# Unit 1's keys ahead of the last two weight conversions, and TensorE in source order from unit 1 on, in a fused complex-decay attention and gated feed-forward kernel

## The chip, the cores and the metric

The kernel runs on one core of one Trainium2 chip. The metric is the device time of one execution in microseconds; the time before is 690.07 us, the median of three runs (689.92 to 690.43). The engines are named as the profile names them: PE is TensorE (PEld its weight loads), DVE is VectorE, ACT is ScalarE, POOL is GpSimd, SP is SyncE, which here only issues DMAs.

## The reference, cut to what matters

```
batch, n_heads, seq, head_dim = (4, 8, 768, 48)
n_tokens, d_model, d_ff = (3072, 384, 1536)
...
mag = np.sqrt(a_re * a_re + a_im * a_im)
scale = np.minimum(mag, 0.999) / (mag + 1e-06)
a_re_n, a_im_n = (a_re * scale, a_im * scale)
for t in range(S):
    new_re = ar * S_re - ai * S_im
    new_im = ar * S_im + ai * S_re
    kv = np.einsum('bhd,bhe->bhde', k[:, :, t], v[:, :, t])
    S_re, S_im = (new_re + kv, new_im)
    y[:, :, t] = np.einsum('bhd,bhde->bhe', q[:, :, t], S_re)
...
a = x @ w_a
b = x @ w_b
return (a * b @ w_out).astype(np.float32)
```

A linear attention whose state is multiplied by a complex decay at each token; its output, 384 wide per token, goes through a gated feed-forward layer of 1536 hidden columns. Everything is fp32.

## The kernel before

**Units.** The 3072 tokens are cut into 12 units of 256 (two batches by a chunk of 128 tokens). Units 0 to 5 are the six chunks of the first pair of batches, 6 to 11 those of the second; a unit carries on the state of the one before it in its six.

**prep(u)**, on DVE with help from ACT, turns the decays of unit u into products over the chunk: about 45 small and large DVE operations in one chain (L205 to L348). In it, scale(u + 1) (L172) prepares the next unit's decays. At its end the queries are multiplied by the products P (times_p, L314) and the keys by a reciprocal (L337), then the second half of times_p follows (for units under LED the query half comes ahead of the reciprocal). stack(u) (L353) then copies queries and keys from the tile qk to the tile stk, ten DMAs on SP's queue a time; for the units under EARLY the query half is stacked in a round of its own, ahead of the keys. load_qk (L350) fetches the next unit's queries and keys into qk after that.

**attn(u)** is PE work: scores (L396), masked by DVE into a tile am (L399); transposes of the keys (L407), copied by ACT into kt (L411); outputs (L436), split by ACT and DVE into two parts xh (L440) and xl (L445); state (L452), added by DVE (L459). A unit in the middle of its six has 2 x 2 scores, 2 x 2 transposes, 2 x 2 outputs and 2 states. They are traced in bundles: the list `order` in attn has a None where one ends. The PSUM tiles of scores, transposes and states take turns on three banks ("m"); am and kt have two buffers each.

**The feed-forward part.** In "window" w, the loop over w at L683, unit w's hidden columns are worked in 12 blocks, k = 0 to 11, two at a time: 36 matmuls of the first layer per pair (L498), the product a*b split into hh and hl by ACT and DVE (L502 to L505, `gated`), and 12 matmuls of the second layer (L534), which lag by one pair. The bundles of attn(w + 1) are traced in the same loop, each after one of the k that SLOTS lists for this w. prep(w + 2) is traced in slices of 2400 ns a k; in window 0 all of prep(2) is traced at k = 11.

**The weights** come as 64-bit numbers and are converted in 12 blocks of three parts, 36 in all: three DVE operations (L142, L144, L146) build a fp32 value in a tile of the name o_sb (three buffers), ACT writes its high part (L150), PE two matmuls with the identity (L152, L153) give the remainder in PSUM, and ACT writes that (L154). Blocks 0 to 5 are traced ahead of unit 0's attention (CONV_FIRST), blocks 6 to 11 in window 0, one a k: at each k the conversion comes first, then a slice of prep(1), and at k = P1_AT = 4 the rest of prep(1), stack(1), eight matmuls of the identity with qk that nothing reads (WARM, L702), load_qk(2).

**What sets the order.** A scheduler reorders each engine's instructions when the kernel is built: what is traced earlier has priority, `high_priority` lifts some of it (the gated operations by 4000, masks and copies of attention by 2000), and a schedule by estimated durations fixes the order. On the chip each engine then runs its own list strictly in that order. Within `tc.manual_schedule(engines={pe.engine})` (L691), PE's list is the order of the source; before, this holds from window w = 4 on (`w + 1 == LED`, LED = 5).

## Time and profile before

| what | value |
|---|---|
| median of three runs | 690.07 us |
| the profiled execution | 688.8 us |
| its span, first to last instruction | 687.1 us |
| granted TensorE clock over the span | 0.974 |
| PE busy | 643.3 us |
| DVE busy | 542.3 us |
| ACT busy | 288.8 us |

A line of a view gives start or group, busy time, count, and in brackets the idle time of that engine just before with what ended it. PE and DVE both run close to without a break from 60 us on; which of them the other waits for differs from stage to stage, so the rows below go by stage.

### The profile page before, as it was taken

The numbers are of one execution on the slowest core, as the hardware profiler recorded it, in microseconds if no ns is written. First come the engines' busy times: TensorE is split into PE (matmuls) and PEld (weight loads), VectorE is DVE, ScalarE is ACT, GpSimd is POOL, SyncE is SP. The second block draws the span as 40 slices with busy tenths as digits, with TensorE's granted clock in tenths as the row PEclk, the third lists the DMA queues.
The fourth block names the chain that finished last, engine by engine and source line by source line (L and its number), as shares of the span: only waits on it lengthen the run. The fifth ranks groups of instructions, "written<-read, shape, count | busy, mean of one in ns | idle before, by whom it ended". The sixth has DMA issues, their size and how long they took to land.

```text
span 687.1 us, 14031 instructions
## 1 busy us (share of the span) xinstructions
PE 643.3 (94%) x5854; PEld 605.4 (88%) x5854; DVE 542.3 (79%) x1069; ACT 288.8 (42%) x472; POOL 5.6 (1%) x11
## 2 busy tenths in 40 slices
PE   3647999999999999999999899999999999999996
PEld 1214889898999999999999899999999899999996
DVE  6999999999989999999998989989989644223221
ACT  7357754634545255352454635346141422221211
POOL 3000000000000000000000000000000000000000
PEclk9577999999999999999999999999999999999999
DMA  8973201512314234061430701520600500400000
GB/s 310 403 297 97 103 1 29 158 55 83 118 37 142 62 100 124 18 183 42 116 123 1 210 30 47 134 75 32 164 29 6 156 32 6 119 24 2 24 1 28
DMA packets 32086, 63.91 MB, mean 93 GB/s; under 512 B 3985, under 2 KB 10641, under 8 KB 32017
## 3 DMA queue, kind: packets, MB, share of 16 engines
q1 hardware_dynamic: 28560, 58.23, 27.3%
q10 hardware_dynamic: 3456, 4.72, 1.9%
q8 instruction: 48, 0.79, 0.5%
q14 instruction: 22, 0.17, 0.1%
HBM read 39.32 MB, written 4.72 MB: 64 GB/s over the span
## 4 chain that ended last, share of the span: by engine, by line
PE 48%; DVE 34%; DMA 7%; ACT 5%; issue 4%; SPq 1%; DVEq 0%; ACTq 0%
PE ab L498 26%; PE o L534 12%; DMA w<-in_dram 5%; PE pm L396 4%; DVE a_t L295 4%; PE xp L436 3%; DVE qk L315 3%; DVE h_t L503 2%; PE pm L452 2%; DVE hl L505 2%; DVE pr L232 2%; DVE z L300 2%; DMA stk<-qk 2%; DVE pr L262 2%; DVE am L399 2%
## 5 line engine op out<-in xcount | busy, mean ns | idle before, releaser
L498 PE MATMUL ab<-xh,w 128*128 128x256 f32 x1728 | 322.5, 281 | 0.1
L498 PEld LDWEIGHTS ab<-xh,w 128*128 128x128 f32 x1728 | 269.8, 188 | 2.1 <-issue 0.6
L498 PE MATMUL ab<-xl,w 128*128 128x256 f32 x864 | 242.1, 280 | 0.2
L498 PEld LDWEIGHTS ab<-xl,w 128*128 128x128 f32 x864 | 162.3, 188 | 1.4 <-DVE xl L445 1.1
L534 PE MATMUL o<-w,hh 128*128 128x384 f32 x576 | 150.4, 341 | 0.0
L503 DVE TENSOR_TENSOR h_t<-ab,h_t 128x512 f32<-128x512 f32 (+1 forms) x73 | 49.5, 678 | 73.9 <-PE ab L498 69.4
L504 ACT CAST hh<-h_t 128x512 fp32r<-128x512 f32 (+1 forms) x73 | 44.7, 612 | 137.5 <-DVE h_t L503 137.4
L534 PEld LDWEIGHTS o<-w,hh 128*128 128x128 f32 x576 | 100.2, 188 | 0.2
L534 PE MATMUL o<-w,hl 128*128 128x384 f32 x288 | 96.9, 337 | 0.0
L502 ACT COPY h_t<-ab 128x512 f32<-128x512 f32 (+1 forms) x73 | 42.0, 576 | 106.6 <-PE ab L498 99.5
L505 DVE TENSOR_TENSOR hl<-h_t,hh 128x512 fp32r<-128x512 f32 (+1 forms) x73 | 49.6, 680 | 13.6 <-ACT hh L504 13.5
L152 PE MATMUL ab<-o_sb,ident 128*128 128x384 f32 x42 | 28.3, 780 | 30.5 <-DVE o_sb L146 20.7
L396 PE MATMUL pm<-stk 128*128 128x128 f32 x384 | 52.8, 279 | 1.9 <-DMA stk<-qk 1.8
L534 PEld LDWEIGHTS o<-w,hl 128*128 128x128 f32 x288 | 54.0, 188 | 0.1
L396 PEld LDWEIGHTS pm<-stk 128*128 128x128 f32 x384 | 47.7, 191 | 5.9 <-issue 2.9
L232 DVE TENSOR_TENSOR pr<-z 128x384 f32<-128x384 f32 (+1 forms) x91 | 47.2, 525 | 2.9 <-ACT z L218 0.9
L152 PEld LDWEIGHTS ab<-o_sb,ident 128*128 128x128 f32 x42 | 9.8, 277 | 39.3 <-DVE o_sb L146 27.0
L295 DVE TENSOR_TENSOR a_t<-z,b_t 128x768 f32<-128x768 f32 x48 | 44.3, 951 | 0.2
L315 DVE TENSOR_TENSOR qk<-qk,z 128x768 f32<-128x768 f32 (+1 forms) x34 | 43.6, 1284 | 0.6
L436 PE MATMUL xp<-am,v_t 128*32 128x128 f32 x768 | 38.1, 276 | 0.5 <-DVE am L399 0.5
L399 DVE TENSOR_TENSOR am<-pm,mask 128x512 f32<-128x512 f32 x48 | 32.1, 683 | 2.3 <-PE pm L396 2.0
L436 PE MATMUL xp<-stk,u 128*32 128x128 f32 x640 | 32.6, 273 | 0.0
(105 smaller groups left out, 745.7 us busy)
## 6 DMA issues: line engine op xcount, KB each, us to landing
w<-in_dram SPq DMA_DIRECT2D x36, 384.0 KB, 8.1
qk<-in_dram SPq DMA_DIRECT2D x12, 768.0 KB, 4.9
a_t<-in_dram SPq DMA_DIRECT2D x11, 768.0 KB, 4.3
stk<-qk SPq DMA_DIRECT2D x42, 192.0 KB, 3.4
v_t<-in_dram SPq DMA_DIRECT2D x24, 256.0 KB, 2.8
out_dram<-o_sb ACTq DMA_DIRECT2D x24, 192.0 KB, 1.9
stk<-qk SPq DMA_DIRECT2D x18, 192.8 KB, 3.3
stk<-qk SPq DMA_DIRECT2D x14, 128.0 KB, 3.1
```

Source lines behind the costliest of these rows:

```text
L232: vec.tensor_tensor(out=pr[:, :, :, o:o + n], in0=view(zz, W + at_(i) + 2 * o, [[W, 2], [-W, 2], [2, n]]), in1=tok(slice(1, 3), i - 1, o, ...
L295: vec.tensor_tensor(out=pz[:, s].rearrange("p (j b e) -> p j b e", j=SUB // 2, e=2), in0=zb[:, 1 + s], in1=view(bb, (1 + k - s) * NB, [[0, ...
L315: vec.tensor_tensor(out=qk4[:, :, k, x0:x1], in0=qk4[:, :, 1, x0:x1], in1=z[:, k].rearrange("p (j t) -> p j t", j=NJ).unsqueeze(2).broadca ...
L396: pe.matmul(out=sp[:, h4], lhsT=stk[:, h, ks], rhs=stk[:, h, qs], start=True, stop=True)
L399: vec.tensor_tensor(out=am, in0=sp, in1=mask[:].unsqueeze(1).broadcast_to([128, 4, 128]), op=ALU.mult)
L436: pe.matmul(out=xp[qd * 32:(qd + 1) * 32, ti], lhsT=l, rhs=rr, start=st, stop=sp_, tile_position=(0, qd * 32), skip_group_check=True)
L498: pe.matmul(out=ab, lhsT=r(w_ab(f, part, m * NJ + i)), rhs=r(xt[:, i, :]), start=n == 0, stop=n == 8)
L502: act.copy(out=h_t, in_=a)
L503: vec.tensor_tensor(out=h_t, in0=b, in1=h_t, op=ALU.mult)
L504: act.copy(out=r(hh), in_=h_t)
L505: vec.tensor_tensor(out=r(hl), in0=h_t, in1=hh, op=ALU.subtract)
L534: pe.matmul(out=os_[tt][:, 0:DM], lhsT=r(ht[:, ts]), rhs=r(w_t[f, 2][:, part, :]), start=(f == 0 and n == 0), stop=(f == NF - 1 and n == 2))
```

## The change

- **HELD = 10.** Blocks 10 and 11 of the weights are traced in `tc.issue_after(done[1].ins)`: on DVE their operations are queued behind the last times_p of unit 1 (`done[u]` is set by each times_p, so its last). It is an order in DVE's list, not a wait.
- In window 0 the conversion of block 6 + k is traced after the slice of prep(1) (and, at k = 4, after stack(1), load_qk(2)), where it was ahead of it.
- **The eight idle matmuls** (L700 to L703) go.
- **LED = 2** where it was 5: PE's list is the source's order from window w = 1 on. What LED also decided in prep (`ahead`) has a name of its own, AHEAD = 5, so nothing changes there.
- **SLOTS.** Window 0 keeps (5, 7, 9, 11); window 1 has (9, 10, 11, 11), window 2 (7, 8, 9, 10), window 3 (5, 6, 7, 9), and from window 4 on (3, 5, 7, 9), where it was (5, 7, 9, 11) in windows 1 and 2, (5, 7, 9, 10) in 3 and (4, 6, 8, 9) from 4 on. The windows ahead of the last chunk of a six keep (5, 7, 9). A k that is named twice has two bundles, with all the second-layer work that is pending between them.
- **The bundles.** Unit 2 has a list of its own; in the units that have no list of their own (all but 0, 2, 5 and 11) the first transposes come between the two first scores.

```
-WARM = 8
+HELD = 10
+AHEAD = 5
-LED = 5
+LED = 2
-SLOTS = ((5, 7, 9, 11), (5, 7, 9, 11), (5, 7, 9, 11), (5, 7, 9, 10), (4, 6, 8, 9))
+SLOTS = ((5, 7, 9, 11), (9, 10, 11, 11), (7, 8, 9, 10), (5, 6, 7, 9), (3, 5, 7, 9))
...
     def split_weights():
         for f in range(NF):
+            with tc.issue_after(done[1].ins) if f >= HELD else nullcontext():
+                split_block(f)
             yield
...
         def times_p(k, x0, x1):
-            vec.tensor_tensor(
+            done[u] = vec.tensor_tensor(
...
-        ahead = u < LED
+        ahead = u < AHEAD
...
+        elif u == 2:
+            order = [(scores, 0, 0), (transposes, 0, 0), None,
+                     (scores, 0, 1), (transposes, 0, 1), (outputs, 0, 0), (outputs, 0, 1), (residual, 0, 0), None,
+                     (scores, 1, 0), (scores, 1, 1), None,
+                     (outputs, 1, 0), (outputs, 1, 1), (residual, 1, 0), (state, 0, 0),
+                     (transposes, 1, 0), (transposes, 1, 1), (state, 1, 0), None]
...
-            order = [(scores, 0, 0), (scores, 0, 1), (transposes, 0, 0), None,
+            order = [(scores, 0, 0), (transposes, 0, 0), (scores, 0, 1), None,
                      (transposes, 0, 1), (outputs, 0, 0), (outputs, 0, 1), (residual, 0, 0), (scores, 1, 0), None,
...
             if w == 0:
-                next(ws, None)
                 drain(p1, P1_F)
                 if k == P1_AT:
                     drain(p1)
                     stack(1)
-                    for i in range(WARM):
-                        wp = bank("m")
-                        pe.matmul(out=wp[:, 0:TOK], lhsT=ident, rhs=qk[:, i % NJ, 1 - i // NJ % 2, TOK:2 * TOK],
-                                  start=True, stop=True)
                     load_qk(2)
                     pgen = prep(2)
+                next(ws, None)
...
             if k in slots:
-                next(at)
+                for n in range(slots.count(k)):
+                    while n and pend:
+                        second()
+                    next(at)
```

More of the change, by code (lines that the diff above doesn't have):

```diff
@@ L1 @@
-from contextlib import ExitStack
+from contextlib import ExitStack, nullcontext
 import concourse.bass as bass
@@ L134, in load_weights @@
                            in_=w_d[f, :, c0:c0 + n].bitcast(U32))
+    done = {}
     def split_weights():
         for f in range(NF):
-            for m, (c0, n) in enumerate(WPART):
-                raw = raws[f, m]
-                t = moe.tile([128, n], F32, name="o_sb", bufs=O_BUFS)
-                tu = t.bitcast(U32)
-                vec.tensor_scalar(out=tu, in0=raw[:, :, 1], scalar1=3, scalar2=0x3FFFFFFF,
-                                  op0=ALU.logical_shift_left, op1=ALU.bitwise_and)
-                vec.scalar_tensor_tensor(out=tu, in0=raw[:, :, 0], scalar=29, in1=tu,
-                                         op0=ALU.logical_shift_right, op1=ALU.bitwise_or)
-                vec.scalar_tensor_tensor(out=tu, in0=raw[:, :, 1], scalar=0xC0000000, in1=tu,
-                                         op0=ALU.bitwise_and, op1=ALU.bitwise_or)
-                w_t[f, m] = wpool.tile([128, 2, n], F32, name=f"w{m}{f}")
-                hi, lo = w_t[f, m][:, 0], w_t[f, m][:, 1]
-                act.mul(out=r(hi), in_=t, mul=-1.0)
-                lp = bank("ab" if f < CONV_ON_AB else "m")
-                pe.matmul(out=lp[:, 0:n], lhsT=ident, rhs=t, start=True, stop=False)
-                pe.matmul(out=lp[:, 0:n], lhsT=r(ident), rhs=r(hi), start=False, stop=True)
-                act.mul(out=r(lo), in_=lp[:, 0:n], mul=-1.0)
@@ L155, in split_weights, with split_block @@
-            yield
+            with tc.issue_after(done[1].ins) if f >= HELD else nullcontext():
+                split_block(f)
+            yield
+    def split_block(f):
+        for m, (c0, n) in enumerate(WPART):
+            raw = raws[f, m]
+            t = moe.tile([128, n], F32, name="o_sb", bufs=O_BUFS)
+            tu = t.bitcast(U32)
+            vec.tensor_scalar(out=tu, in0=raw[:, :, 1], scalar1=3, scalar2=0x3FFFFFFF,
+                              op0=ALU.logical_shift_left, op1=ALU.bitwise_and)
+            vec.scalar_tensor_tensor(out=tu, in0=raw[:, :, 0], scalar=29, in1=tu,
+                                     op0=ALU.logical_shift_right, op1=ALU.bitwise_or)
+            vec.scalar_tensor_tensor(out=tu, in0=raw[:, :, 1], scalar=0xC0000000, in1=tu,
+                                     op0=ALU.bitwise_and, op1=ALU.bitwise_or)
+            w_t[f, m] = wpool.tile([128, 2, n], F32, name=f"w{m}{f}")
+            hi, lo = w_t[f, m][:, 0], w_t[f, m][:, 1]
+            act.mul(out=r(hi), in_=t, mul=-1.0)
+            lp = bank("ab" if f < CONV_ON_AB else "m")
+            pe.matmul(out=lp[:, 0:n], lhsT=ident, rhs=t, start=True, stop=False)
+            pe.matmul(out=lp[:, 0:n], lhsT=r(ident), rhs=r(hi), start=False, stop=True)
+            act.mul(out=r(lo), in_=lp[:, 0:n], mul=-1.0)
```

## The prediction

> **What bounds the kernel now.** I began with the page's busy times.
>
> ```profile
> span 687.1 us, 14031 instructions
> PE 643.3 (94%) x5854; PEld 605.4 (88%) x5854; DVE 542.3 (79%) x1069; ACT 288.8 (42%) x472; POOL 5.6 (1%) x11
> ```
>
> PE is at work 94% of the span, so a gain has to come from PE's idle or useless time. To find it I cut the span at each unit's first first-layer matmul. Columns: stretch and length, then busy time (count) of PE, PEld, DVE, ACT, POOL, the granted clock, DMA share, GB/s.
>
> ```profile
> 77.59:143.18 65.59, 65.05 (x546) 58.33 (x545) 63.23 (x136) 38.59 (x69) 0.00 (x0) 1.00 0.20 58
> 143.18:195.78 52.60, 51.15 (x499) 49.78 (x498) 48.56 (x103) 21.91 (x34) 0.00 (x0) 1.00 0.26 79
> 195.78:246.47 50.69, 50.59 (x499) 49.21 (x498) 47.09 (x88) 22.53 (x34) 0.00 (x0) 1.00 0.27 81
> 246.47:296.62 50.15, 50.07 (x500) 49.09 (x498) 47.21 (x84) 22.96 (x34) 0.00 (x0) 1.00 0.34 102
> ...
> 342.81:393.00 50.19, 48.41 (x433) 47.32 (x433) 45.96 (x91) 26.43 (x42) 0.00 (x0) 1.00 0.36 105
> ...
> 493.27:544.91 51.64, 50.44 (x497) 49.13 (x497) 45.13 (x84) 18.21 (x28) 0.00 (x0) 1.00 0.22 63
> 544.91:594.74 49.83, 49.83 (x497) 49.18 (x497) 17.75 (x24) 11.08 (x20) 0.00 (x0) 1.00 0.24 67
> ```
>
> The same work, some 500 matmuls, takes 49.83 us in window 9, where PE never waits, and the clock is granted in full throughout. Windows 1, 2, 3 and 8 are 2.8, 0.9, 0.3 and 1.8 us longer. Window 5 has 64 matmuls fewer and is yet no shorter. In windows 0 to 3 DVE is as full as PE (63.23 of 65.59 us, 48.56 of 52.60), so keys may come late there. Next, PE in order of time around attn(1), and the longest waits later:
>
> ```profile
> 123.02 3.72 PE L702 MATMUL pm<-qk,ident 128*128 128x256 f32 x16
> 126.58 0.81 PE L152 MATMUL pm<-o_sb,ident 128*128 128x384 f32 x2
> ...
> 129.03 1.89 PE L396 MATMUL pm<-stk 128*128 128x128 f32 x14
> 131.29 0.49 PE L396 MATMUL pm<-stk 128*128 128x128 f32 x2 [0.36 <-DMA stk<-qk]
> ...
> 170.94 0.49 PE L396 MATMUL pm<-stk 128*128 128x128 f32 x2 [1.45 <-DMA stk<-qk]
> ...
> 383.19 0.55 PE L407 MATMUL pm<-ident,stk 96*128 96x96 f32 x4 [1.31 <-DVE am L399]
> ...
> 534.72 0.55 PE L407 MATMUL pm<-ident,stk 96*128 96x96 f32 x4 [1.12 <-DVE am L399]
> ```
>
> From 123.02 to 126.58 PE runs matmuls that nothing reads, then converts block 11 until 129.03, and only then scores unit 1. At 170.94 it waits for unit 2's stacked keys; at 383.19 and 534.72 (windows 5 and 8) for a mask. So unit 1 and 2 wait for keys, that is for DVE; the last two wait for the place of one DVE operation.
>
> **Part one: the conversions behind the keys.** DVE in that stretch:
>
> ```profile
> 97.39 0.19 DVE L262 TENSOR_TENSOR pr<-c_t,b_t 128x24 f32<-128x24 f32 x1
> 97.50 0.35 DVE L142 TENSOR_SCALAR o_sb<-w 128x384 uint32<-128x384 uint32 x1
> ...
> 114.44 0.62 DVE L142 TENSOR_SCALAR o_sb<-w 128x384 uint32<-128x384 uint32 x2
> 114.98 1.01 DVE L144 SCALAR_TENSOR_TENSOR o_sb<-w,o_sb 128x384 uint32<-128x384 uint32 x2
> ...
> 119.54 0.95 DVE L337 TENSOR_TENSOR qk<-qk,a_t 128x768 f32<-128x768 f32 x1
> ...
> 121.74 0.35 DVE L142 TENSOR_SCALAR o_sb<-w 128x384 uint32<-128x384 uint32 x1
> 122.01 0.95 DVE L315 TENSOR_TENSOR qk<-qk,z 128x768 f32<-128x768 f32 x1
> ...
> 124.22 0.55 DVE L146 SCALAR_TENSOR_TENSOR o_sb<-w,o_sb 128x384 uint32<-128x384 uint32 x1
> ```
>
> The last six of the 36 L142, those of blocks 10 and 11, run from 97.50 to 121.74. Two L142 take 0.62 and two L144 1.01, so in a full list one costs 0.27 and 0.47; L146 is as long as L144. Ahead of the last L315 at 122.01 stand 6 L142, 5 L144 and 5 L146: 1.6 + 4.7 = 6.3 us. Not all of it is won, since some fills the latency between dependent small operations:
>
> ```profile
> 146.42 0.20 DVE L262 TENSOR_TENSOR pr<-c_t,b_t 128x24 f32<-128x24 f32 x1
> 146.66 0.18 DVE L264 TENSOR_TENSOR b_t<-pr 128x12 f32<-128x12 f32 x1
> ...
> 162.14 0.96 DVE L329 TENSOR_TENSOR a_t<-a_t 128x768 f32<-128x768 f32 x1 [1.00 <-ACT a_t L311]
> ...
> 165.60 1.95 DVE L315 TENSOR_TENSOR qk<-qk,z 128x768 f32<-128x768 f32 x2
> ```
>
> In unit 2's chain the next operation follows an L262 after 0.24 us; with a conversion between it was 0.11. Some nine such places give back 1.1 us, and the wait for ACT (1.00 at 162.14), which conversions hid in unit 1, up to 0.9. I take 1.8 us back and the keys 4.5 us earlier: done at 118.5 rather than 122.97. The ends are 0 (all of it fill) and 6.3.
>
> SP's queue comes next:
>
> ```profile
> 114.55 7.00 SPq L363 DMA_DIRECT2D stk<-qk  x10
> ...
> 122.99 6.47 SPq L363 DMA_DIRECT2D stk<-qk  x10
> ...
> 167.58 8.32 SPq L363 DMA_DIRECT2D stk<-qk  x10
> ```
>
> The query half is issued from 114.55 to 121.55. It comes forward by block 10's share of 2.5 us, to end at 119.05, so the keys' ten DMAs start there and not at 118.5: SP takes 0.5 of the gain. Their issue takes 6.5 us, and the last data arrived 1.8 us after it (131.29 against 129.46), so unit 1 is stacked by 127.4.
>
> PE's work by piece, from the chain of waits, and the first-layer matmuls (busy time and count of PE and PEld) that it did of the last pair ahead of 123.02:
>
> ```profile
> 588.47 4.31 PE ab L498 x36
> 592.78 2.12 PE o L534 x12
> ...
> 613.91 1.78 PE pm L396 x16
> ...
> 622.06 1.89 PE xp L436 x64
> ```
>
> ```profile
> 117.95:123.02 5.07, 3.21 (x22) 2.67 (x22) 1.00 0.52 121
> ```
>
> A pair is 4.24 + 2.12 = 6.36 us (36 matmuls at 0.118 us, the 4.31 containing a start, and two second-layer blocks); six are 38.2, which leaves 11.6 of 49.83 for attention. PE loses its useless 3.56 us and the wait of 0.36. But it also runs dry: block 10's three conversions (2.45 us, by block 11's from 126.58 to 129.03) move behind the keys, and so do the 22 matmuls (2.6 us) of the last pair, which needs them. PE is out of work at 123.02 - 2.45 - 2.6 = 118.0. From there 20.8 us are left (the pair's 4.24, six conversions 4.9, attn(1) 11.6). Idle time until the first conversion is through DVE and ACT and the first keys are there, some 2.2 us, puts the start of window 1 at 141.0, not 143.18. The ends are 138.8 (no idle time) and 143.2.
>
> **Part two: window 1.** The conversions removed ahead of unit 1's keys, 6.3 us, and the 0.94 that already stood behind them are now queued ahead of prep(2). DVE has the same work up to unit 2's keys as before, and those end at 167.55 (L315 at 165.60, 1.95 us). Only what was fill and is now idle is added, 1.8 us, less what conversions can fill in prep(2): I take keys(2) at K = 168.5, with 165.3 (all idle time filled) and 174.8 (all 7.25 us added) as ends.
>
> With PE in source order and SLOTS (9, 10, 11, 11), the first scores of unit 2 stand after five pairs. Five pairs make 31.8: PE reaches the first bundle at 172.8. The data for its four heads, half of the ten DMAs, is there at K + 4.2 + 1.8 = 174.5, a wait of 1.7 us. The second bundle follows a half pair (4.24 us) and the first bundle's last 0.5 us later, at K + 10.8 = 179.3; the last head landed at K + 8.32 + 1.8 = 178.6, in time. From there all is PE work: half the scores 0.9, outputs 2 x 1.89, other scores 1.78, four second-layer blocks 4.24, transposes and states 3.7, together 14.4, and 0.5 us for masks, since scores and outputs stand close here. Window 2 starts at K + 25.7 = 194.2. By work alone it would be 141.0 + 49.8 = 190.8, so keys decide, and what window 0 gains is mostly absorbed. **Gain at window 2: 1.6 us.** This term has the widest ends: +5.0 where keys come at 165.3, -4.7 at 174.8.
>
> **Part three: windows 2 to 4.** PE in source order loses nothing to interleaving, so windows 2 and 3 should take 49.83: 0.86 + 0.32 = **1.2 us**. The keys must be there. Unit 3's were ready 44.6 us after unit 2's:
>
> ```profile
> 210.22 1.95 DVE L315 TENSOR_TENSOR qk<-qk,z 128x768 f32<-128x768 f32 x2
> ```
>
> (212.17 against 167.55), so at 213.1, four heads stacked at 219.1. The bundle after k = 7 stands four pairs into window 2, at 219.6. It just holds. Window 3's stands three pairs in, at 263.1; with 44.6 us more, four heads are there at 263.7, a wait of 0.6 at most. The end on the poor side is 0 or a wait of 1 us in each. Window 4 keeps bundles and order: nothing.
>
> **Part four: windows 5 to 10.** The third and fourth bundle stood at k = 8 and 9, with 2.12 us of second-layer matmuls between; now at 7 and 9, with 6.36. The mask that PE waited for 1.31 and 1.12 us then has three times as long. Both waits go: **2.4 us**. What is late next there is the copy of the transposes by ACT, which the states wait for inside the last bundle; it stays. A wait can also turn up elsewhere, as DVE's list is laid anew: 0 to 3.
>
> **The sum.** 1.6 + 1.2 + 2.4 = 5.2 us. The profiled execution took 688.8, 1.7 beyond its span; it becomes 683.6. It is 1.27 below the median, to which the same 5.2 apply: 684.9.
>
> [...] The idle matmuls stand where PE would be idle. The rows of the start:
>
> ```profile
> 54.00:57.58 3.58, 1.08 (x3) 0.48 (x3) 3.58 (x7) 2.78 (x6) 0.00 (x0) 0.98 0.21 56
> 57.58:64.41 6.83, 5.61 (x9) 2.90 (x10) 6.28 (x14) 5.56 (x10) 0.00 (x0) 0.50 0.41 101
> ```
>
> After 3.58 us with PE busy for 1.08, the next 6.83 us were granted half the clock. [...]
>
> **Rivals.**
> *The clock falls* after 118. Half the clock for 6.83 us costs up to 3.4 us before window 1, at 144.4. By work window 2 then starts at 194.2, and the keys' 194.2 hides it: 684.9 where they do, 688.3 where they came early, say 686.5. Against it: the conversions that arrive each 1.2 us.
>
> *PE becomes the bound at once.* If conversions fill DVE's idle time and K is 165.3 or less, window 2 starts at 190.8, 5.0 earlier, and the rest holds: 5.0 + 1.2 + 2.4 = 8.6, 681.5; 679 if the smaller waits of windows 5 to 8 go too.
>
> *No net effect.* The scheduler lays DVE's list so that the masks and gated operations wait as before, and source order costs what it saves: 690.
>
> *Slower.* The conversions were only fill. The chain of dependent operations sets DVE's pace, unit 1's keys gain little, and 7.25 us stand ahead of prep(2). PE being ahead puts one more gated product ahead of them:
>
> ```profile
> L503 DVE TENSOR_TENSOR h_t<-ab,h_t 128x512 f32<-128x512 f32 (+1 forms) x73 | 49.5, 678 | 73.9 <-PE ab L498 69.4
> ```
>
> K becomes 175.5, window 2 starts at 201.2, 5.4 late, as source order lets nothing past the waiting scores. Then 5.4 - 1.2 - 2.4 = 1.8 slower: 691.9. It decides from K of about 175. For it: DVE's list was full by count. Against: 0.11 us a place against 0.47 for an operation.
>
> **How the numbers follow.** Forecast 0.50, PE-bound 0.22, clock 0.08, no net effect 0.08, slower 0.12. A measurement can tell some 0.2% (1.4 us) from no change: the first three are faster, 0.80; 0.08 the same; 0.12 slower. The range runs from 679.0, where all waits go, to 690.0, which leaves out the slower case and little else.
>
> **What would show it.** Right: no L702; the last L315 of unit 1 near 118.5; first scores near 122; window 1 from 141; unit 2's keys near 168.5; windows 2 and 3 at 49.8 to 50; no L407 waiting for a mask in windows 5 and 8. Wrong: unit 2's keys past 173, a PEclk of 0.5 after 117, or waits for masks over 1 us inside windows 1 to 3.

## The result, and the profile after

The changed kernel takes **694.84 us** (median of nine runs, 692.27 to 696.06) against 690.8 us for the kernel before in the same session (nine runs): a ratio of **1.0057, 95% interval 1.0040 to 1.0074**. The forecast was 684.9 us, with a range up to 690.0: wrong in sign. The profiled execution took 693.78 us.

The page of the changed kernel, span and busy times:

```profile
span 692.1 us, 14005 instructions
PE 644.0 (93%) x5838; PEld 607.4 (88%) x5838; DVE 544.1 (79%) x1069; ACT 289.3 (42%) x472; POOL 5.6 (1%) x11
```

Sixteen of PE's instructions are gone (5838 for 5854: the eight idle matmuls are sixteen there), and yet PE's busy time is 0.7 us more and the span 5.0 us more. Where, the table by windows shows, cut as before at each unit's first first-layer matmul (stretch and length, busy time and count of PE, PEld, DVE, ACT, POOL, clock, DMA share, GB/s):

```profile
77.48:145.03 67.55, 63.53 (x531) 56.81 (x529) 63.95 (x134) 38.34 (x69) 0.00 (x0) 0.95 0.19 56
145.03:202.63 57.60, 54.47 (x512) 52.84 (x510) 53.86 (x112) 23.41 (x37) 0.00 (x0) 0.97 0.26 78
202.63:251.59 48.96, 48.04 (x488) 47.29 (x486) 45.46 (x85) 22.82 (x33) 0.00 (x0) 1.00 0.28 82
...
347.27:399.77 52.50, 50.09 (x433) 49.02 (x433) 48.21 (x96) 27.77 (x43) 0.00 (x0) 0.97 0.39 115
...
499.63:549.55 49.92, 49.92 (x497) 49.22 (x497) 41.46 (x88) 14.70 (x24) 0.00 (x0) 1.00 0.24 66
```

| windows | predicted, after less before | measured |
|---|---|---|
| 0 | -2.2 | **+1.97** |
| 1 and 2 together | -0.3 | **+3.27** |
| 3 and 4 | -0.3 | -0.66 |
| 5 | -1.3 | **+2.31** |
| 6 and 7 | 0 | -0.41 |
| 8 | -1.1 | -1.72 |
| 9 and 10 | 0 | +0.10 |
| sum | -5.2 | +4.86 |

(Windows 1 and 2 stand together, because 12 matmuls have passed from the one to the other: 512 and 488 for 499 and 499.) Windows 3, 4 and 8 went the way that was forecast. Window 0, windows 1 and 2 taken together, and window 5 went the other way, and in windows 0, 1 and 5 the granted clock is below 1.00, where it was 1.00 before.

**Window 0.** The changed kernel's PE in order of time:

```profile
117.22 0.34 PE L547 MATMUL o<-w,hl 128*128 128x384 f32 x1
121.32 1.65 PE L160 MATMUL pm<-o_sb,ident 128*128 128x384 f32 x2 [3.76 <-DVE o_sb L154]
122.19 1.09 PE L161 MATMUL pm<-w,ident 128*128 128x384 f32 x1
...
129.38 0.81 PE L160 MATMUL pm<-o_sb,ident 128*128 128x384 f32 x2
...
130.20 1.05 PE L403 MATMUL pm<-stk 128*128 128x128 f32 x8
```

PE ran dry at 117.56, close to the 118.0 of the forecast. But it waited 3.76 us for DVE's first held conversion, not 2.2; it then ran block 10's three conversions at half the clock (1.09 for an L161, where block 11's at 128.91 took 0.63 at the full clock); and the scores, which the forecast had near 122, stand in PE's list behind both blocks' conversions and came at 130.20. They have no bracket: their keys had long been there. SP's row says since when:

```profile
119.35 6.41 SPq L370 DMA_DIRECT2D stk<-qk  x10
```

The issue ends at 125.76; with the 1.8 us that the last data took before, the keys are stacked by 127.6 (the last of these DMAs landed at 127.50). So the keys did come early, and nothing used it. DVE, which PE waits for, in the same stretch:

```profile
112.98 0.69 DVE L516 TENSOR_TENSOR h_t<-ab,h_t 128x512 f32<-128x512 f32 x1 [1.04 <-ACT a_t L317]
113.92 0.96 DVE L336 TENSOR_TENSOR a_t<-a_t 128x768 f32<-128x768 f32 x1 [0.24 <-ACT a_t L318]
...
117.37 1.95 DVE L322 TENSOR_TENSOR qk<-qk,z 128x768 f32<-128x768 f32 x2
119.25 0.62 DVE L150 TENSOR_SCALAR o_sb<-w 128x384 uint32<-128x384 uint32 x2
...
127.61 1.02 DVE L154 SCALAR_TENSOR_TENSOR o_sb<-w,o_sb 128x384 uint32<-128x384 uint32 x2
```

Unit 1's keys end at 119.32 (117.37 + 1.95), 3.64 us earlier than the 122.96 of before. The last conversion ends at 128.63 (127.61 + 1.02), against 124.77 before (the L146 at 124.22). From window 0's start to that end, first before, then changed:

```profile
77.60:124.77 47.17, 46.99 (x307) 42.21 (x306) 45.98 (x105) 26.14 (x49) 0.00 (x0) 1.00 0.13 36
```

```profile
77.48:128.63 51.15, 47.13 (x293) 41.68 (x292) 48.24 (x106) 27.98 (x51) 0.00 (x0) 0.93 0.19 53
```

DVE does the same operations in both stretches, and in the changed kernel one more, a product of prep(2) that takes some 0.5 us in a full list. The stretch is 3.98 us longer (51.15 against 47.17); without that operation it is 3.5. Of these, 1.7 us are idle (51.15 - 48.24, against 47.17 - 45.98), of which the 1.04 and 0.24 for ACT above are the largest new pieces. The other 1.8 are inside the busy time; my reading is that a small operation that waits for the one before it no longer has a conversion running beside its end (in the changed kernel, behind the L269 at 97.31 a conversion begins after 0.12 us, while the L269, of 0.19, still runs; behind the one at 98.50, of 0.20, the operation that reads its product begins after 0.23). The conversions were fill, 3.5 us of it.

In PE's own terms nothing was saved: its 3.72 us of useless work became a wait of 3.76. The 1.97 us that window 0 grew are busy time (63.53, against 65.04 - 3.72 = 61.32 of useful work before), much of it block 10's conversions at half the clock. Even so the clock is not what held the scores: they stand behind the last conversion, and PE took that one up at 129.38, 0.75 us after DVE had it ready. A faster PE could have had the scores no more than 0.75 us earlier.

**Window 1.** PE got to unit 2's first bundle at 177.15 and to the second at 182.64, without a wait for keys. Then, on PE, the outputs of the second bundle, and DVE's list ahead of the mask that they wait for:

```profile
182.64 1.05 PE L403 MATMUL pm<-stk 128*128 128x128 f32 x8
...
184.41 0.40 PE L443 MATMUL xp<-am,v_t 128*32 128x128 f32 x6
187.68 0.33 PE L443 MATMUL xp<-am,v_t 128*32 128x128 f32 x1 [2.87 <-DVE am L406]
```

```profile
184.00 0.96 DVE L203 SCALAR_TENSOR_TENSOR sc<-a_t,sc 128x768 f32<-128x768 f32 x1
184.87 0.68 DVE L516 TENSOR_TENSOR h_t<-ab,h_t 128x512 f32<-128x512 f32 x1
185.47 0.95 DVE L205 SCALAR_TENSOR_TENSOR sc<-sc,a_t 128x768 f32<-128x768 f32 x1
186.34 0.69 DVE L518 TENSOR_TENSOR hl<-h_t,hh 128x512 fp32r<-128x512 f32 x1
186.94 0.69 DVE L406 TENSOR_TENSOR am<-pm,mask 128x512 f32<-128x512 f32 x1
```

The mask's scores were done by 183.7 (182.64 + 1.05). DVE is never idle; the mask simply has four large operations of other work ahead of it in a list that was fixed when the kernel was built.

**Window 5.** The wait for the mask (1.31) is gone, and another one, small before, has grown. First PE before, then PE and ACT's list in the changed kernel:

```profile
386.03 0.88 PE L452 MATMUL pm<-v_t,kt 128*96 128x48 f32 x8 [0.47 <-ACT kt L411]
```

```profile
386.92 0.49 PE L414 MATMUL pm<-ident,stk 96*128 96x96 f32 x4
...
388.35 0.88 PE L459 MATMUL pm<-v_t,kt 128*96 128x48 f32 x8
391.13 0.88 PE L459 MATMUL pm<-v_t,kt 128*96 128x48 f32 x8 [1.90 <-ACT kt L418]
```

```profile
388.44 0.62 ACT L517 CAST hh<-h_t 128x512 fp32r<-128x512 f32 x1
389.78 0.94 ACT L192 ACTIVATE sc<-a_t,biases 128x768 f32<-128x768 f32 x1 [0.72 <-DVE a_t L191]
390.62 0.46 ACT L418 COPY kt<-pm 128x384 f32<-128x384 f32 x1
```

The transposes were there at 387.4. Their copy stands behind other work of ACT, the last piece of which itself waits 0.72 us for DVE.

**The clock.** The changed kernel's clock in the 3.41 us ahead of each fall, and behind it:

```profile
116.14:119.55 3.41, 1.42 (x9) 1.10 (x7) 3.31 (x6) 0.00 (x0) 0.00 (x0) 1.00 0.37 93
119.55:122.96 3.41, 1.64 (x3) 1.03 (x4) 3.41 (x9) 1.04 (x3) 0.00 (x0) 0.50 0.87 289
122.96:126.37 3.41, 3.41 (x9) 2.18 (x8) 3.29 (x8) 3.09 (x5) 0.00 (x0) 0.50 0.54 140
184.40:187.81 3.41, 0.54 (x18) 0.27 (x14) 3.38 (x7) 1.00 (x2) 0.00 (x0) 1.00 0.02 6
187.81:191.22 3.41, 3.41 (x45) 2.99 (x42) 2.48 (x10) 0.48 (x1) 0.00 (x0) 0.50 0.02 5
389.20:392.61 3.41, 1.51 (x16) 1.48 (x16) 3.27 (x8) 2.83 (x6) 0.00 (x0) 1.00 0.80 203
392.61:396.02 3.41, 3.41 (x19) 3.41 (x18) 3.11 (x7) 2.27 (x4) 0.00 (x0) 0.50 0.49 128
```

In each of the three waits a stretch with PE busy for 1.51 us or less is followed by one at half the clock. Where PE has work to do then (187.81, 392.61), it does less of it: from 393.00 to 394.92 a first-layer matmul (L511) began every 0.213 us, from 396.48 to 397.54, at the full clock, every 0.118. At these rates 3.41 us at half the clock do what takes 1.9 us at the full one, so by this estimate such a wait costs up to 1.5 us once more.

### The profile page after: what moved, and what is told of

Read it like the earlier page. It is cut to its first block, busy times and chain, and to the rows that moved or that the text cites. A ratio compares the mean times of both kernels' runs of the same rounds, so it can differ in the third digit from the quotient of the medians.

```text
span 692.1 us, 14005 instructions
## 1 busy us (share of the span) xinstructions
PE 644.0 (93%) x5838; PEld 607.4 (88%) x5838; DVE 544.1 (79%) x1069; ACT 289.3 (42%) x472; POOL 5.6 (1%) x11
## 4 chain that ended last, share of the span: by engine, by line
PE 65%; DVE 24%; ACT 4%; DMA 3%; issue 3%; SPq 0%; DVEq 0%; ACTq 0%
PE ab L511 32%; PE o L547 16%; PE pm L403 5%; PE xp L443 5%; PE pm L459 3%; DMA w<-in_dram 3%; DVE qk L322 2%; DVE a_t L302 2%; DVE h_t L516 2%; DVE hl L518 2%; PE pm L414 1%; DVE z L307 1%; DVE pr L239 1%; DVE o_sb L152 1%; PE ab L160 1%
## 5 line engine op out<-in xcount | busy, mean ns | idle before, releaser
L511 PE MATMUL ab<-xh,w 128*128 128x256 f32 x1728 | 323.1, 282 | 0.5 <-DVE h_t L516 0.5
L511 PEld LDWEIGHTS ab<-xh,w 128*128 128x128 f32 x1728 | 271.0, 189 | 2.2 <-DVE h_t L516 0.7
L511 PE MATMUL ab<-xl,w 128*128 128x256 f32 x864 | 242.7, 281 | 0.0
L511 PEld LDWEIGHTS ab<-xl,w 128*128 128x128 f32 x864 | 163.2, 189 | 0.5 <-DVE xl L452 0.2
L547 PE MATMUL o<-w,hh 128*128 128x384 f32 x576 | 148.7, 339 | 0.0
L459 PEld LDWEIGHTS pm<-v_t,kt 128*96 128x96 f32 x320 | 29.2, 165 | 5.8 <-ACT kt L418 3.5
```

The costliest lines, as they stand in the source:

```text
L459: pe.matmul(out=kp[0:KS, h * D:(h + 1) * D], lhsT=kts[i, h // 4][:, h % 4, :], rhs=v_t[:, o:o + D], start=True, stop=True)
L511: pe.matmul(out=ab, lhsT=r(w_ab(f, part, m * NJ + i)), rhs=r(xt[:, i, :]), start=n == 0, stop=n == 8)
L547: pe.matmul(out=os_[tt][:, 0:DM], lhsT=r(ht[:, ts]), rhs=r(w_t[f, 2][:, part, :]), start=(f == 0 and n == 0), stop=(f == NF - 1 and n == 2))
```

## The experiments

The theories. The first (S in the expectations, where it is named) was that block 10's absence starves PE in window 0, and that the change's other half would still gain. Its rivals: that the conversions were fill on DVE, so that any holding back, of one block or two, makes DVE's list longer; that the loss is the clock's; and that the new order costs by itself (O). M is a later one, on unit 1's first mask in DVE's list. The table gives the median, the ratio to the kernel before with its interval, and from each profiled execution window 0, the time from the start of window 0 to that of window 3, window 5, and to the start of window 11 (lengths of the windows added up). The medians are of several sessions, in which the kernel before took 689.4 to 690.8 us, so medians are compared by the ratios. A single profiled execution has its own scatter: before, late_only and late_st1 have the same lists on DVE and ACT in window 0, and take 65.58, 65.57 and 66.36 us there; changed, u2_gap and after_mended, alike in the same way, take 67.55, 67.08 and 67.47. A difference under some 0.8 us between two traces tells nothing by itself.

| kernel | median us | ratio, 95% | window 0 | to window 3 | window 5 | to window 11 |
|---|---|---|---|---|---|---|
| before | 690.8 | 1 | 65.58 | 168.87 | 50.19 | 562.97 |
| changed | 694.84 | 1.0057 (1.0040-1.0074) | 67.55 | 174.11 | 52.50 | 567.83 |
| keys_alone | 693.61 | 1.0046 (1.0027-1.0065) | 67.19 | 171.03 | 50.75 | 566.19 |
| order_alone | 691.85 | 1.0028 (1.0014-1.0041) | 66.44 | 172.42 | 51.01 | 564.73 |
| held11 | 694.97 | 1.0073 (1.0050-1.0097) | 68.80 | 175.94 | 53.00 | 570.79 |
| held12 | 689.29 | 0.9985 (0.9969-1.0002) | 67.18 | 170.31 | 51.99 | 564.15 |
| idle_back | 691.77 | 1.0038 (1.0020-1.0056) | 66.94 | 171.92 | 51.58 | 564.86 |
| no_idle | 693.51 | 1.0061 (1.0038-1.0083) | 66.02 | 170.29 | 50.39 | 565.26 |
| mask_held | 688.99 | 0.9993 (0.9976-1.0011) | 68.38 | 171.30 | 49.81 | 564.45 |
| u2_gap | 692.99 | 1.0060 (1.0028-1.0092) | 67.08 | 172.42 | 52.97 | 567.09 |
| late_only | 689.57 | 1.0006 (0.9980-1.0032) | 65.57 | 169.18 | 50.94 | 562.00 |
| late_st1 | **686.18** | **0.9951** (0.9934-0.9969) | 66.36 | 169.60 | 48.18 | 560.16 |
| order_mended | 688.22 | 0.9980 (0.9968-0.9992) | 65.67 | 170.28 | 49.59 | 561.49 |
| after_mended | 690.35 | 1.0002 (0.9984-1.0020) | 67.47 | 172.64 | 49.70 | 563.64 |

### The two halves apart: keys_alone and order_alone

keys_alone is the changed kernel with the old order: the conversions held, the idle matmuls gone.

```
-LED = 2
+LED = 5
-SLOTS = ((5, 7, 9, 11), (9, 10, 11, 11), (7, 8, 9, 10), (5, 6, 7, 9), (3, 5, 7, 9))
+SLOTS = ((5, 7, 9, 11), (5, 7, 9, 11), (5, 7, 9, 11), (5, 7, 9, 10), (4, 6, 8, 9))
...
-        elif u == 2:
...
-            order = [(scores, 0, 0), (transposes, 0, 0), (scores, 0, 1), None,
+            order = [(scores, 0, 0), (scores, 0, 1), (transposes, 0, 0), None,
```

> The first part alone: blocks 10 and 11 held behind unit 1's keys, no idle matmuls, the conversion traced after the slice of prep(1); PE's order, SLOTS and bundles as before. Theory S (the held conversions leave TensorE without work at the end of window 0 and the clock halves): window 1 starts near 145, about 1.9 us later than before, a PEclk of 0.5 for 6.8 us from some 119, and, as the scheduler's order hides some of it, 1 to 3 us slower than before in all. Theory O (source order from unit 1 on is what costs, by masks and copies that stand too late in VectorE's and ScalarE's lists): this part by itself is no slower than before, 687 to 691 us.

order_alone is the kernel before with the new order: LED = 2, the new SLOTS and bundles; conversions and idle matmuls as before.

```
+AHEAD = 5
-LED = 5
+LED = 2
...
+SLOTS = ((5, 7, 9, 11), (9, 10, 11, 11), (7, 8, 9, 10), (5, 6, 7, 9), (3, 5, 7, 9))
...
+        elif u == 2:
...
+            order = [(scores, 0, 0), (transposes, 0, 0), (scores, 0, 1), None,
```

> The second part alone: LED 2 with AHEAD 5, the new SLOTS and bundles; conversions and idle matmuls as before. Theory O: a wait for a mask of 2 to 4 us in window 1's outputs, unit 3's window some 3 us later than before, a wait of 2 us for a copy of the transposes in window 5, 1.7 us won in window 8: 2 to 4 us slower than before. Theory S: window 1 starts at 143.2 as before, and with the start in time the new order saves what the prediction counted, 2 to 4 us faster than before.

Both are slower, by 0.46% and 0.28%. By the start of window 3 the keys' half has lost 2.16 us and the order's half 3.55; together 5.71, where the whole change lost 5.24; by window 11 it is 3.22 and 1.76, together 4.98, for 4.86. So the two halves add, near enough, and neither hides a gain of the other. Each of the theories in the expectations is right on one half and wrong on the other: S had order_alone faster than before, O had keys_alone no slower. PE's wait in keys_alone, in the place where the changed kernel waited 3.76:

```profile
122.55 1.65 PE L160 MATMUL pm<-o_sb,ident 128*128 128x384 f32 x2 [3.79 <-DVE o_sb L154]
```

The same, with the old order. And order_alone, whose conversions are those of before, in window 1:

```profile
185.80 0.30 PE L437 MATMUL xp<-am,v_t 128*32 128x128 f32 x1 [2.58 <-DVE am L400]
```

The wait for unit 2's mask belongs to the new order, not to the held conversions.

### How many blocks are held: held11 and held12

held11:

```
-HELD = 10
+HELD = 11
```

held12, by which nothing is held:

```
-HELD = 10
+HELD = 12
```

Both are otherwise the changed kernel, without the idle matmuls.

> The changed kernel with HELD = 11: block 10 is converted as it comes, block 11 alone waits behind unit 1's keys; no idle matmuls. Theory S says that it is block 10 that TensorE lacks: the wait of 3.9 us before its conversions goes, window 1 starts 1 to 2 us earlier than in the changed kernel (67.5 us after window 0), unit 1's keys end 1 to 2.5 us later than its 119.3. In all 0.5 to 2 us faster than the changed kernel. If the late start of window 1 comes from the scheduler's order of conversions and scores and not from the missing block, window 1 starts as late as there.

> The changed kernel with HELD = 12, so that no conversion is held; no idle matmuls either, all else as changed. Theory S: TensorE has block 10's conversions and 22 first-layer matmuls to do while unit 1's keys are made, it is idle for under 2 us, the clock stays whole and window 1 starts at 141 to 143: 2 to 4 us faster than the changed kernel, 0 to 2 slower than before. Theory O: what is lost from window 1 on stays, so under 1 us is won against the changed kernel.

If PE were only starved of block 10, holding block 11 alone would have mended it. held11 is no faster than the change; by its ratio, from four runs, and by its trace it is the slowest of all. Its PE:

```profile
124.59 0.91 PE L160 MATMUL pm<-o_sb,ident 128*128 128x384 f32 x2 [1.79 <-DVE o_sb L154]
...
128.53 0.81 PE L403 MATMUL pm<-stk 128*128 128x128 f32 x4 [2.03 <-DMA stk<-qk]
```

One wait has become two, for the conversion 1.79 and then for the keys 2.03, 3.82 in sum. held12 waits only for the keys:

```profile
129.16 0.46 PE L403 MATMUL pm<-stk 128*128 128x128 f32 x2 [2.82 <-DMA stk<-qk]
```

So S falls in this form. In each variant PE is idle or does useless work for 2.5 to 4.5 us here (before: 3.56 of idle matmuls and a wait of 0.36; the ends are no_idle and idle_back, below), under whatever name. I read this so: DVE sets the end of this stage, and the place of the conversions only decides which of its products is the late one. held12, 0.9985 against the change's 1.0057, is faster than the change; against the kernel before no difference can be told. That time is near what S gave for it, but not for S's reason: PE waited 2.82 us where S had under 2, the clock fell to 0.50 from 130.25 to 133.66, and window 0 is no shorter than 67.18.

### The idle matmuls: idle_back and no_idle

idle_back puts the eight idle matmuls back into the changed kernel; they read the query half of qk, so that they need not wait for the keys.

```
+                    for i in range(WARM):
+                        wp = bank("m")
+                        pe.matmul(out=wp[:, 0:TOK], lhsT=ident, rhs=qk[:, i % NJ, 1 - i // NJ % 2, 0:TOK],
+                                  start=True, stop=True)
```

> The changed kernel with the eight idle matmuls back, reading the query half of qk, which is ready some 5 us earlier, so that they stand ahead of the time without work and not in it. It tells what the fallen clock is worth by itself: the conversions of block 10 still come when they come. Theory S with the clock as the main part: no PEclk of 0.5 between 117 and 127, block 10's six conversions in 2.5 us and not 5, window 1 at 142 to 143, 1.5 to 2.5 us faster than the changed kernel. If the missing work and not the clock is the main part: under 1 us faster.

no_idle takes them out of the kernel before, with nothing else changed.

```
-WARM = 8
...
-                    for i in range(WARM):
-                        wp = bank("m")
-                        pe.matmul(out=wp[:, 0:TOK], lhsT=ident, rhs=qk[:, i % NJ, 1 - i // NJ % 2, TOK:2 * TOK],
-                                  start=True, stop=True)
```

> The kernel before without the eight idle matmuls, and nothing else. If they only cost their 3.6 us, unit 1's scores start when the keys land, near 127, and window 1 starts 1.5 to 3.5 us earlier: faster by as much, less what the late keys of unit 2 take back. If they hold the clock, TensorE's idle time after 123 brings a PEclk of 0.5 for 3.4 us or more, and window 1 starts within 1 us of before: no faster than before.

idle_back's window 0, and PE at the matmuls and at the first conversion:

```profile
77.73:144.67 66.94, 65.94 (x547) 58.21 (x545) 61.98 (x130) 39.00 (x69) 0.00 (x0) 1.00 0.20 57
```

```profile
111.11 3.72 PE L715 MATMUL pm<-qk,ident 128*128 128x256 f32 x16 [0.43 <-DVE qk L323]
...
122.17 0.88 PE L161 MATMUL pm<-o_sb,ident 128*128 128x384 f32 x2 [0.35 <-DVE o_sb L155]
```

With 3.72 us of useless work in it and the clock at 1.00, window 0 takes 66.94 instead of 67.55: PE's useless time did not lengthen it, and no_idle says the same the other way round, for without the useless work window 0 of the kernel before takes 66.02 instead of 65.58, and PE waits 2.46 us for the keys. The clock in window 0 is worth 0.6 us by this comparison. (The scheduler laid DVE's list differently too, and 0.6 is within the scatter; the 0.75 us above is the firmer bound.)

no_idle is slower than the kernel before, by 0.61%. Its profiled execution has a clock of 1.00 all through windows 0 to 10 and still reaches window 11 2.29 us later than before, so these 2.29 are not the clock; of the rest that its timed runs lost, the trace says nothing. Its DVE:

```profile
127.30 0.36 DVE L237 TENSOR_TENSOR z<-pr 128x192 f32<-128x192 f32 x1
130.44 0.69 DVE L398 TENSOR_TENSOR am<-pm,mask 128x512 f32<-128x512 f32 x1 [2.79 <-PE pm L395]
```

DVE itself stands still for 2.79 us, for unit 1's first scores. Without the idle matmuls the scheduler queued the first mask behind the first product step of prep(2) (the L237 at 127.30 ends it), where it was the fourth before. Presumably its estimates, without the time of the idle matmuls, had the scores come earlier; no run here shows the estimates.

With order_alone, idle_back, held12 and the changed kernel all four cases stand under the new order, but for two differences: the last three also trace the conversion after the slice of prep(1), and idle_back's idle matmuls read the queries. To window 11: both as before 564.73, only held 564.86, only the idle matmuls gone 564.15, both 567.83. The ratios agree with it: 1.0028, 1.0038, 0.9985, 1.0057. Neither edit measurably costs by itself there; the two together cost 3.1 us by the traces, of which 1.11 lie in window 0, 0.58 in windows 1 and 2, and 1.49 in window 5 (52.50 against order_alone's 51.01). DVE's list is laid anew in each, so parts this small do not add cleanly. The 1.49 are a fall of the clock after a wait that order_alone has too (last section), and so may be chance.

### Unit 1's first mask: mask_held

Theory M: that place of the mask is what no_idle lost. mask_held is no_idle with the mask queued behind the fourth step again; for that, prep(2)'s first steps are traced at k = 4, which is a second edit.

```
-            with tc.high_priority(offset=ATTN_FIRST):
+            held = tc.issue_after(done[2, MASK_AT].ins) if (u, i, hg) == (1, 0, 0) else ExitStack()
+            with tc.high_priority(offset=ATTN_FIRST), held:
...
+                    while (2, MASK_AT) not in done:
+                        next(pgen)
```

> The kernel before without the idle matmuls, as no_idle, and with one order more: on VectorE unit 1's first mask is queued behind the fourth step of prep(2)'s products, where it stands in the kernel before, and not behind the second (prep(2)'s first steps are traced at k = 4 for that). Theory M: the idle matmuls are worth something because the scheduler, with them, sets the scores and so their masks later; without them the mask stands so early in VectorE's list that VectorE waits 2.8 us for the scores, and unit 2's keys end 4.5 us later. Then here that wait goes, unit 2's keys end at 90 to 92 us after the start of window 0 (no_idle 94.5, before 90.0), and the whole is 1.5 to 4 us faster than no_idle, 0 to 2 slower than before. If it is the clock or TensorE's missing work that counts, unit 2's keys stay at 94 and the time stays where no_idle's is.

(The expectation's "second" step is the first, as the line at 127.30 showed.) By the medians M holds: 0.9993 against 1.0061, and the intervals do not meet. By the trace it does not show. DVE's wait of 2.79 us for the scores goes, but others come (1.48 us for ACT, 0.94 for the next scores), and unit 2's keys end 94.03 us after the start of window 0, where M had 90 to 92 and its rival 94. Window 0 is longer, not shorter (68.38 against 66.02; the clock fell in it, to 0.98 in the mean), and to the start of window 3 it gains nothing (171.30 against 170.29); the whole is 0.8 us shorter where the medians say 4.5. So what no_idle lost through the mask's place is not shown. What the timed runs of no_idle did that its profiled one did not stays open.

### Unit 2's bundles: u2_gap

In the changed kernel, unit 2's first outputs move behind the next second-layer work, so that their masks have time.

```
-                     (scores, 0, 1), (transposes, 0, 1), (outputs, 0, 0), (outputs, 0, 1), (residual, 0, 0), None,
-                     (scores, 1, 0), (scores, 1, 1), None,
+                     (scores, 0, 1), (transposes, 0, 1), None,
+                     (outputs, 0, 0), (outputs, 0, 1), (residual, 0, 0), (scores, 1, 0), (scores, 1, 1), None,
```

> The changed kernel, where unit 2's outputs of the first half move from the second bundle to the third, so that 2.1 us of second-layer matmuls stand between the scores and the outputs that need their mask. VectorE's list is the same around that mask. If the wait of 3.1 us in window 1 is for the place of the mask in VectorE's list, it shrinks by what now stands between, to about 1 us, and window 3 starts some 2 us earlier than in the changed kernel, counted from the start of window 0 (174.1 us there). If TensorE waits there for unit 2's keys or for something else that comes late as such, the wait moves and window 3 starts as in the changed kernel.

```profile
186.62 0.30 PE L443 MATMUL xp<-am,v_t 128*32 128x128 f32 x1 [0.89 <-DVE am L406]
...
198.41 1.63 PE L459 MATMUL pm<-v_t,kt 128*96 128x48 f32 x16 [2.16 <-DVE u L466]
```

The wait for the mask falls from 2.87 to 0.89 and one of 2.16 appears in the last bundle, for DVE's addition of the first state. Start of window 3 at 172.42 instead of 174.11, but window 5 half a microsecond longer, and the ratio, 1.0060 with its wide interval, is that of the change: not a gain that can be told.

### The late windows: late_only and late_st1

late_only is the kernel before with the new slots and the new order of bundles from window 5 on only (and the slots for window 4).

```
-SLOTS = ((5, 7, 9, 11), (5, 7, 9, 11), (5, 7, 9, 11), (5, 7, 9, 10), (4, 6, 8, 9))
+SLOTS = ((5, 7, 9, 11), (5, 7, 9, 11), (5, 7, 9, 11), (5, 7, 9, 10), (3, 5, 7, 9))
...
-            order = [(scores, 0, 0), (scores, 0, 1), (transposes, 0, 0), None,
+            order = [(scores, 0, 0)] + ([(scores, 0, 1), (transposes, 0, 0)] if u < LED else [(transposes, 0, 0), (scores, 0, 1)]) + [None,
```

> The kernel before with the last entry of SLOTS (3, 5, 7, 9) for (4, 6, 8, 9) and the new bundle order in units 6 to 10 alone: the prediction's fourth part by itself. The waits of 1.3 and 1.1 us for a mask in windows 5 and 8 go. By the trace of the changed kernel window 8 then takes 49.9 us and not 51.6, while window 5 gets a wait of 2 us for a copy of the transposes: 1 to 2 us faster than before. If window 5's wait is of the changed kernel's early windows (its lists laid from another start), it does not come here and the gain is 2.5 to 4 us.

By the medians it is level with the kernel before, with an interval too wide for the gain that was expected; by the trace it is 0.97 us faster. Window 8's 1.72 us come, and window 5 gives 0.75 back.

```profile
387.74 0.88 PE L452 MATMUL pm<-v_t,kt 128*96 128x48 f32 x8 [2.60 <-ACT kt L411]
```

late_st1 adds one thing: unit 6's last state gets a bundle of its own after k = 10, behind a pair of first-layer blocks, so that the copy has time.

```
-                     (transposes, 1, 1), (outputs, 1, 0), (outputs, 1, 1), (residual, 1, 0), (state, 1, 0), None]
+                     (transposes, 1, 1), (outputs, 1, 0), (outputs, 1, 1), (residual, 1, 0), *([None] if c == 0 else []),
+                     (state, 1, 0), None]
...
+        if w + 1 < NU and (w + 1) % NCH == 0:
+            slots += (10,)
```

> late_only with unit 6's last state moved from the fourth bundle, after k = 9, to a bundle of its own after k = 10, so that 4.2 us of first-layer matmuls stand between the transposes and the state that needs their copy. If window 5's wait of 2.8 us there is for the place of the copy in ScalarE's list alone, it goes, and window 5 takes 48 us and not 50.9: 2 to 3 us faster than late_only and 2.5 to 4 than before. If the copy waits for something that comes late as such, the wait stays or moves to the next unit's start and the gain on late_only is under 1 us.

```profile
343.44:391.62 48.18, 48.18 (x434) 47.48 (x434) 44.95 (x90) 25.98 (x40) 0.00 (x0) 1.00 0.34 103
```

Window 5 takes 48.18 with PE never idle, 2.0 less than before. At 0.9951 this is the fastest version, and its interval lies clear of 1. It holds only what the prediction's part four promised, with its late copy mended.

### All mended: order_mended and after_mended

order_mended is order_alone with the edits of u2_gap and late_st1; after_mended is the changed kernel with the same two.

> order_alone (conversions and idle matmuls as before, TensorE in source order from window 1 on) with the two bundles mended: unit 2's first outputs a bundle later, unit 6's last state a bundle later. order_alone was 1.8 us slower than before by its trace; the waits of 2.8 us for a mask in window 1 and of 2.1 us for a copy in window 5 go but for 1 us: 1 to 3 us faster than before. If source order costs by itself in windows 1 and 2, it stays no faster than before.

> The changed kernel with both of the bundles that were found to make TensorE wait mended: unit 2's first outputs a bundle later, unit 6's last state a bundle later; held conversions and missing idle matmuls as in the change. If the waits in windows 1 and 5 and the held conversions are separate terms: window 5 (52.50 in the changed kernel) takes 48 to 49.6, window 1 about 56, 2.5 to 4 us less than the change in all: 691 to 692, and what is left above the kernel with only the order mended (688.2) is the held part, 2 to 4 us, all of it in windows 0 and 1 (start of window 3 at 171 to 173 us after window 0's start, against 170.28 there). If the held part only cost because the order behind it was rigid: 688 to 689, level with the kernel with only the order mended.

order_mended, 0.9980, is a little faster than the kernel before, but windows 1 and 2 take 104.61 us against 103.29 before, so the source's order from unit 1 on is still worse than the scheduler's there. Its remaining wait is again that for DVE's addition of the state:

```profile
197.16 1.60 PE L453 MATMUL pm<-v_t,kt 128*96 128x48 f32 x16 [2.17 <-DVE u L460]
```

after_mended, 1.0002, is 0.0022 above it by the ratios, 1.5 us, and the two intervals just touch. By the traces it is 2.36 us later at the start of window 3 and 2.15 at window 11, 1.80 of it in window 0. Of its two expectations the first, separate terms, fits the trace (window 1 55.77, window 5 49.70, window 3 from 172.64); the median lies between the two. So some 2 us are the price of the keys' half once the order's two waits are out. So the account of the change's 4.86 us, by the traces: 2.2 to 3.2 for the conversions held and the idle matmuls gone together (after_mended, keys_alone), the rest for the order; with the order's two bundles mended, 4.19 of the 4.86 are gone (563.64 against 567.83), and what the kernel then still loses in windows 0 to 2 (3.77 us to the start of window 3) it wins back in the late ones, 3.10.

## Why the prediction was wrong, point by point

**Part one, "PE loses its useless 3.56 us and the wait of 0.36."** This is the step that failed first. I counted PE's useless matmuls as time on the path, though DVE was as full as PE in that window and the last conversion on DVE stood ahead of everything that PE had left to do. The trace showed PE dry for 3.76 us without them, and idle_back and no_idle showed that they cost nothing.

**"Not all of it is won ... I take 1.8 us back and the keys 4.5 us earlier."** The mechanism was right and the size off: the keys came 3.64 us earlier, so 2.7 were given back ahead of them; up to the last conversion it is 3.5. I priced the gaps between small operations and one wait for ACT; the list gave back twice that.

**"Idle time until the first conversion is through DVE and ACT and the first keys are there, some 2.2 us."** It was 3.76; above all, this treats the rest of PE's work as ready then. The held conversions left DVE one by one until 128.63, and in PE's list the scores stand behind all of them. An early operand is worth nothing where its consumer is queued behind a later one: the keys were stacked by 127.50, as forecast (127.4), and the first score began at 130.20, behind the last conversion. Window 1 began at 145.03, not 141.0.

**Part two, "0.5 us for masks".** The other term of the sum that was mis-sized: 2.87 us in the changed kernel, 2.58 with the order alone. The keys of unit 2, on which the part turned, ended at 170.01 (168.5 forecast) and held PE up nowhere; the five pairs ahead of its first bundle took 32.1 us (31.8 forecast). I also set window 2 at 49.83 and window 1's end without the second-layer pair that moves into it (512 matmuls), which changes the boundary and not the sum.

**Part three.** Windows 3 and 4 gained 0.66, and window 2, by its matmul count, lost little: 0.92 of idle time. Right in kind.

**Part four, "Both waits go: 2.4 us."** They went. In window 8 that gave 1.72. In window 5 the step failed at its own last sentence, "What is late next there is the copy of the transposes by ACT ... it stays": it was named and charged nothing, and it grew from 0.47 to 1.90 us; with the fall of the clock behind it the window is 2.31 longer. late_st1 shows what the term would have been with it mended: 2.0 in window 5.

**The rival of the clock** was right that it falls (0.50 from 119.55 to 126.37), and in window 0 right that little hangs on it. What I did not see is that it would fall in windows 1 and 5 too, after waits of 2.87 and 1.90 us, and the sum had no term for that. Window 5 shows the price alone: changed kernel and order_alone both wait 1.90 us there for the same copy, one with a clock of 0.97 and 52.50 us, the other at 1.00 and 51.01. Half a clock for 3.41 us is 1.5 us here, almost as much as the wait. Window 1 has the same 0.97.

**The rival "slower"** named the fill, rightly, and its threshold wrongly: it was to decide by unit 2's keys past 175, and they never mattered. That the order would cost 3.55 us by itself, through a mask and the clock behind it, was in no case: "no net effect" said that the masks wait as before, and one waited longer. The likely reason is that the scheduler had been free to put other PE work in front of waiting outputs and the source's order was not; u2_gap, where some 2 us of second-layer work in front take 1.98 off that wait, fits it.

## What to carry to other kernels

When two engines are both full in a stage, find the last product that the stage's end hangs on and follow the list of the engine that makes it; useless work on the other engine is a sign of slack there, not a gain to collect (here 3.72 us became a wait of 3.76). Moving operations out of a chain of small dependent ones takes away its fill (here 3.5 us), so count what the same operations take in sum, not what is taken out ahead of one result. And before an engine's order is fixed by hand, give each result that another engine must return (a mask, a copy, an addition) a piece of independent work between the request and the use: one bundle more for one state, with the late slots, made the kernel 0.5% faster.

## What the runs showed of the hardware

**The granted clock fell behind some of PE's waits.** Between 65 and 645 us the fourteen traces of the table were cut into pieces of 3.41 us, from 64.93 on in the changed kernel. The clock of each piece is 1.00 or 0.50, with nothing between. At 0.50 there are 14 single pieces and four pairs (6.83 us) in ten of the traces, and none in before, no_idle, late_only and late_st1. Pieces of order_alone: the one in window 1 after which its clock fell, and the two around its wait of 1.90 us in window 5:

```profile
183.56:186.97 3.41, 1.17 (x41) 1.17 (x42) 3.27 (x9) 1.00 (x2) 0.00 (x0) 1.00 0.02 7
384.95:388.36 3.41, 2.45 (x46) 1.98 (x44) 3.30 (x6) 2.61 (x4) 0.00 (x0) 1.00 0.84 217
388.36:391.78 3.42, 2.48 (x23) 2.48 (x24) 3.25 (x9) 3.39 (x7) 0.00 (x0) 1.00 0.83 222
```

The 1.90 us there lie half in one piece and half in the next, with PE busy for 2.45 and 2.48 us, and the clock stayed at 1.00; in the changed kernel they fell into one piece (389.20 to 392.61, 1.51 busy) and the next was at 0.50. In all fourteen traces 12 pieces at the full clock had PE busy for less than 1.60 us, and the next piece was at 0.50 each time; 15 had 1.60 to 2.00, and the next was at 0.50 after 6 of them (1.68 to 1.99) and at 1.00 after 9 (1.60 to 2.00); behind more than 2.00 none fell. (Of the four pairs, the first piece had PE busy for 1.55, 1.61, 1.64 and, in held11 from 201.48, 3.00.) These counts are all that the traces show; what decides between the 6 and the 9 is not in them. So the same wait of 1.90 us went with 1.5 us more in window 5 of the one kernel and with nothing more in the other.

**A filler can order other engines.** This is the scheduler's doing, not the chip's. The eight idle matmuls served nothing in time, and yet the kernel before was 0.6% slower without them (no_idle). What is seen to change is DVE's list: without them the first mask of unit 1 stands behind the first product step of prep(2), with them behind the fourth, and DVE stood still for 2.79 us. That the mask's place is the whole of the loss is not shown (mask_held).
